# Sliding-window attention into a cosine-gated MLP on one core: register loads, the fifth half batch's key and query loads, w_out and three sets of casts placed elsewhere in the order

## The chip, the core and the metric

The kernel runs on one core of a Trainium2 chip. The metric is the device time of one execution in microseconds (us); the time of a kernel is the median of its runs. A profile is one execution more, recorded by the hardware profiler. Engines: PE (TensorE, matmuls; PEld is its weight load), DVE (VectorE), ACT (ScalarE), POOL (GpSimd, which also issues the DMAs that change the type) and SP (SyncE, which here issues DMAs only). Each engine works through its own instructions in the order in which they were written down.

## What is computed

Attention over 8 batches, 8 heads, 576 tokens and a head dimension of 64. A token sees its neighbours within 32 positions, and 8 global tokens see all and are seen by all. The result goes through an MLP whose hidden layer is multiplied by its own cosine.

```python
scores = scale * q @ k^T                       # where |i - j| <= 32, or i or j is global; else -1e9
attn   = exp(scores - max) / sum               # softmax
x      = (attn @ v), heads joined              # 4608 x 512
h      = x @ w_in                              # 512 -> 2048
out    = (h * cos(h)) @ w_out                  # 2048 -> 512, float32, 4608 x 512
```

## The kernel before

Work is cut into pairs of heads: 4 pairs make a batch, 2 a half batch, so there are 32 pairs and 16 half batches (s = 0 to 15; pair pr belongs to half batch pr // 2). The first five half batches (pairs 0 to 9) are loaded as they are and turned on PE; from half batch 5 on, keys, queries and values are first cast to fp16 in DRAM and then read with transposing DMAs. The MLP runs over 9 tiles of 512 tokens, each in 16 steps of the first product (four matmuls 128x512 into `ph`, L771, a cosine on ACT, L777, and a product on DVE that makes `g`, L778) and 16 steps of the second (four matmuls into `po`, L809).

**Who sets the order.** Nothing is scheduled by a tool: the order of every engine's instructions is written out by hand as strings of steps. FRONT holds the first five half batches; the loop then runs one round for each s from 4 on: MID for s = 4, FIFTH for s = 5, SIXTH for s = 6, ORDER for the others. A step calls one function, which appends its instructions to each engine that it uses. Steps that matter here, with what they issue:

- `sN`, `pN`, `xN`: scores of pair N (PE `st` L640, ACT `e` L643 and L647, DVE `pm` L644 and L648); values (PE `pv` L655, DVE `dg`, `r_all` and `xn`, L669 to L675); transposes of xn (PE `tx` L687, DVE `xT` and `xg`, L688 to L693), and after the fourth pair of a batch eight POOL copies of the global columns into xT (L696; L761 from pair 10 on), each at a column that a register holds. From pair 10 on the same steps are L708 to L717, L728 to L739 and L753 to L756. In the round strings, `sa`, `sz`, `pa`, `pz`, `xa`, `xz` are the two pairs of the round's half batch, and `kc qc`, `kd qd` bring the next half batch's keys and queries into `kw` and `qb` (L616, L628 on DVE).
- `kN qN` in FRONT: keys and queries of pair N turned on PE (L604) and copied by ACT (L613 to L625).
- `L4`: POOL issues the loads of half batch 4's keys and queries (L282, `kn` and `qn`). `M4`: SP issues its value rows (`vn`, L376, five loads, and two small ones, L381). `C2`, `C3`, `C4`: POOL casts the value rows of half batch 2, 3 or 4 into `vw` (L411, `cast_vn`). For s = 2 and 3 a one-element copy into `gate` comes first (L409): it reads the newest mask product `pm`. There are two buffers of `pm`, so the DVE product of the pair after the next has to wait for that copy.
- `I`: two iotas (L954, L955) and the reading of the eight global positions into POOL's registers (L956).
- `W0` to `W3`: POOL issues the four quarters of w_in (L902). `O`: w_out (L906), 2 MB in fp16, into a tile whose first part held keys and queries of half batch 2 until then. `H2`: a cast of the global values.
- `K5`, `K6`, `K7`: POOL issues the fp16 casts of half batch 5, 6 or 7 in DRAM (k and q at L273, v at L269). `V10`, `V12`: a one-element POOL copy (L398) that waits for `qb` of that pair and so holds back the casts behind it. From round 6 on, `G` does the same for later half batches (a copy that waits for xn, L988, then the casts).
- `B5`, and `bring(s + 2)` at the end of a round: SP issues the transposing loads of keys and queries (L287, L288), which wait for the casts, and the value loads into `vw` (L353 to L360, L423).
- `Z0` to `Z4`: DVE builds the mask of the later half batches in five parts; `Z5` clears the edges of `kT` and `qT`. `A0` to `A2`: gathers of the global rows on POOL (L338). `1` and `2`: one step of the MLP's first or second product; `m` and `t` are the two halves of a `1`. `f4`: four filling matmuls. `n`: a sum of squares on ACT (L827).

SP also stores each output block (L818), in the order in which the blocks and the `bring` steps were written. Three buffers hold blocks that wait for their store.

Of the kernel before, what the change touches and what calls it, by code (L numbers as in the profile page):

```python
# [20 lines left out]
NP = H // 2  # L21
# [25 lines left out]

ORDER = "2 kz qz sa 2 2 2 sz pa 1 2 1 2 xa n pz 1 1 G 2 xz 1 1 2 kc qc 1 1"

MID = ("+ 1 1 1 1 Z0 1 1 1 Z1 1 1 Z2 1 1 A0 1 Z3 1 1 1 n1 Z4 1 1 A1 1 1 1 Z5 A2 1 1 1 B5 1 2 2 g10 g11 kc qc V10 K6 n2 2 2 1 1 2 2 n3 kd qd - 2 2")  # L50

FIFTH = "sa G 2 2 2 2 sz pa 1 1 2 xa pz 2 2 2 kc qc V12 K7 xz n kd qd"

SIXTH = "sa 2 2 2 2 sz pa 1 1 2 xa 1 1 pz G 2 xz n 1 1 D0 2 kc qc D1 1 D2 2 1"

FRONT = ("M1 s0 E0 C0 E1 L2 w6 k1 q1 w4 s1 y0.0 f8 k2 q2 C1 H0 p0 M2 L3 y0.1 s2 k3 q3 f4 x0 p1 M3 s3 H1 g4 g5 g6 C2 g7 L4 I k4 q4 f4 x1 p2 M4 s4 "
         "C3 W0 k5 q5 f4 x2 p3 s5 g8 g9 W1 W2 W3 k6 q6 f4 x3 p4 s6 C4 k7 q7 f4 x4 p5 n0 s7 k8 q8 f4 x5 p6 s8 H2 k9 q9 f4 x6 p7 s9 "
         "x7 p8 O m m x8 K5 p9 t t + m m t t x9 -")
WARM = 13
KQ = 80  # L60
OK_ALL = float(P * (B * NP * 2 * BP + B))
# [144 lines left out]
def kernel(  # L206
# [189 lines left out]
    def hold(pr):  # L396

        nc.gpsimd.tensor_copy(gate, qb[pr % NK][0:1, 0, G : G + 1])  # L398

    def hold_x(pr):  # L400

        nc.gpsimd.tensor_copy(gate, xn_of[pr // 2][0:1, pr % 2, 0, 0:1])
# [2 lines left out]
        return view(vw[s % NV], (4 * (D + 1), NK5), (D + 1, 4), (1, D + 1))  # L405

    def cast_vn(s):
        if 1 < s < 4:
            nc.gpsimd.tensor_copy(gate, pm_of[max(pm_of)][0:1, 2 * CN - 1 : 2 * CN])  # L409
        old, new = vn_of(s).rearrange("p t (h d) -> p t h d", h=4), vn16(s)  # L410
        nc.gpsimd.tensor_copy(new[:, :, :, 0:D], old)  # L411
# [497 lines left out]
    with tc.manual_schedule():  # L909
# [85 lines left out]
        def bring(s):  # L995
# [4 lines left out]

        LOCAL = {"k": local_k, "q": local_q}
        OTHER = LOCAL | {"g": globals_kq, "L": load_qk, "W": load_w_in, "v": load_values, "n": x_squares,
                 "C": cast_vn, "I": row_numbers, "E": early_rows, "w": lambda n: warm(n, "h" if n == 6 else "s"), "y": value_rows, "M": next_values, "S": spread_vg, "V": hold, "U": hold_x, "H": early_globals, "Z": steady_buffers, "f": fill, "r": load_vn, "A": later_rows, "D": later_globals, "O": load_w_out, "K": lambda s: cast_half(s, "kqv"), "B": bring, "m": lambda _: one(False), "t": lambda _: mlp_act()}
        ready[0] = 1
        for step in FRONT.split():
            if step in "+-":
# [5 lines left out]
        for s in range(4, B * NP // 2):  # L1012
# [25 lines left out]
                        f(pr, *[int(x) for x in step[2:]])  # L1038
            if s % 2 == 1:
                ready[0] = s // 2 + 1 + (s // 2 == B - 1)  # L1040
            if 3 < s < B * NP // 2 - 2:
                bring(s + 2)
        x_squares(B * NP // 2 - 1)
        make_identity(nc, ident)
# [48 lines left out]
```

## Time and profile before

| | us |
|---|---|
| median of 3 runs (348.47 to 351.66) | 350.42 |
| the profiled execution | 351.74 |
| its span, first to last instruction | 349.9 |
| PE busy in the span | 328.1 |
| DVE busy | 249.7 |
| ACT busy | 238.3 |
| POOL busy | 106.1 |

The profile gives busy times of each engine, the waits with what ended them, a timeline, and the clock that PE was granted. The profiled execution took 351.74 us, of which 349.9 us are the span; 1.8 us lie around it. A row of a timeline reads: start in us, duration, engine, line, operation, out<-in, count, and in brackets how long the engine had been idle before it and what ended that.

### The profile page before, as it was taken

What the parts mean: (1) busy time and instruction counts of PE and PEld (TensorE: products, weight loads), DVE (VectorE), ACT (ScalarE), POOL (GpSimd) and SP (SyncE); (2) the same over time, 40 slices, a digit from 0 to 9 for tenths busy, and PEclk for the clock granted to TensorE, in tenths of its full rate; (3) what the DMA queues carried; (4) which work ended last, traced back from release to release, by engine and by line L of the source; (5) the groups of instructions that cost most, each with busy time, mean ns of one, the idle gap of its engine ahead of it and who ended that gap; (6) DMA issues with size and microseconds to landing.
All of it is one profiled execution on the core that took longest, in us unless ns stands there. A gap on an engine that the chain in (4) does not pass through costs nothing.

```text
span 349.9 us, 8348 instructions
## 1 busy us (share of the span) xinstructions
PE 328.1 (94%) x3153; PEld 170.9 (49%) x3153; DVE 249.7 (71%) x610; ACT 238.3 (68%) x411; POOL 106.1 (30%) x217
## 2 busy tenths in 40 slices
PE   6988589999998899999999999999999999999993
PEld 2567475444453345545454545454545444444452
DVE  6579768996575778888887978787888566556310
ACT  4887766885765686969687877778787866644300
POOL 7844737435043505250705071415001000000000
PEclk9999969999998999999999999999999999999997
DMA  5999995999999999999999999999990001100112
GB/s 86 195 151 166 176 204 71 197 179 94 209 98 181 156 175 130 186 131 164 165 199 147 184 135 182 139 182 142 178 130 7 30 32 51 39 33 30 60 62 68
DMA packets 165763, 45.00 MB, mean 129 GB/s; under 512 B 153060, under 2 KB 160868, under 8 KB 165540
## 3 DMA queue, kind: packets, MB, share of 16 engines
q1 hardware_dynamic: 106244, 26.86, 55.3%
q0 software_dynamic: 59472, 17.54, 49.3%
q8 instruction: 27, 0.44, 0.5%
q14 instruction: 20, 0.16, 0.2%
HBM read 44.93 MB, written 19.17 MB: 183 GB/s over the span
## 4 chain that ended last, share of the span: by engine, by line
PE 84%; DMA 4%; DVE 3%; ACT 3%; POOL 2%; issue 2%; SPq 1%; POOLq 0%; ACTq 0%
PE ph L771 36%; PE po L809 32%; PE pv L728 3%; PE st L708 2%; DMA qn<-in_q_dram 2%; PE tx L753 2%; PE pv L655 2%; DMA kn<-in_k_dram 2%; PE bank L604 1%; PE po L791 1%; PE pv L502 1%; PE tx L687 1%; PE st L640 1%; DVE g L778 1%; PE t L322 1%
## 5 line engine op out<-in xcount | busy, mean ns | idle before, releaser
L771 PE MATMUL ph<-xT,w_in 128*128 128x512 f16 x576 | 140.6, 383 | 2.5 <-POOL xT L761 1.7
L777 ACT ACTIVATE cos<-ph,pio 128x512 f16<-128x512 f32 x144 | 97.6, 687 | 61.2 <-PE ph L771 58.9
L809 PE MATMUL po<-w_out,g 128*128 128x512 f16 x560 | 136.9, 379 | 0.0
L778 DVE TENSOR_TENSOR g<-cos,ph 128x512 f16<-128x512 f16 x144 | 96.7, 686 | 47.5 <-ACT cos L777 44.9
L771 PEld LDWEIGHTS <-w_in 128*128 128x128 f16 x576 | 54.3, 98 | 64.5 <-issue 3.7
L809 PEld LDWEIGHTS <-g 128*128 128x128 f16 x560 | 53.7, 98 | 63.8 <-issue 0.6
L711 ACT ACTIVATE e<-st 128x512 f16<-128x512 f32 x44 | 23.9, 594 | 9.2 <-PE st L708 9.0
L712 DVE TENSOR_TENSOR pm<-e,mask 128x512 f16<-128x512 f16 x44 | 18.8, 429 | 13.5 <-ACT e L711 12.0
L988 POOL COPY gate<-xn 1x1 f16<-1x1 f16 x8 | 1.5, 182 | 82.3 <-DVE xn L739 82.3
L761 POOL COPY xT<-xg 128x4 f16 x48 | 17.2, 358 | 30.2 <-DVE xT L756 27.6
L273 POOL DMA_DIRECT2D q<-in_q_dram x11 | 24.3, 2212 | 0.0
L827 ACT ACTIVATE xn<-xn 128x1536 f16<-128x1536 f16 (+1 forms) x16 | 22.7, 1417 | 0.0
L739 DVE TENSOR_TENSOR xn<-pv,r_all 128x768 f16<-128x768 f32 x22 | 21.1, 958 | 1.0
L814 ACT COPY o<-po 128x512 f32<-128x512 f32 x17 | 10.0, 586 | 13.4 <-PE po L809 13.4
L816 DVE COPY o<-po 128x512 f32<-128x512 f32 x18 | 12.4, 690 | 9.2 <-PE po L809 8.7
L273 POOL DMA_DIRECT2D k<-in_k_dram x11 | 18.1, 1644 | 1.4 <-issue 1.4
L777 ACT ACT_TABLE_LOAD x12 | 15.4, 1283 | 0.2
L643 ACT ACTIVATE e<-st 128x488 f16<-128x488 f32 x20 | 10.6, 575 | 7.2 <-PE st L640 6.5
L711 ACT ACT_TABLE_LOAD x11 | 14.1, 1283 | 0.2
L644 DVE TENSOR_TENSOR pm<-e,qT 128x488 f16<-128x488 f16 x20 | 10.5, 551 | 4.8 <-issue 2.4
L708 PEld LDWEIGHTS <-kw 64*128 64x128 f16 x484 | 8.4, 95 | 9.9 <-issue 7.7
L588 POOL COPY kw<-kgT 128x88 f16<-128x88 f16 x22 | 12.7, 757 | 0.0
(182 smaller groups left out, 380.1 us busy)
## 6 DMA issues: line engine op xcount, KB each, us to landing
out_dram<-o SPq DMA_DIRECT2D x35, 256.0 KB
vw<-v SPq DMA_DIRECT2D x32, 165.0 KB
k<-in_k_dram POOLq DMA_DIRECT2D x11, 288.0 KB, 8.4
q<-in_q_dram POOLq DMA_DIRECT2D x11, 288.0 KB, 10.8
v<-in_v_dram POOLq DMA_DIRECT2D x11, 288.0 KB, 5.0
vn<-in_v_dram SPq DMA_DIRECT2D x20, 120.0 KB
w_in<-in_moe_w_in_dram POOLq DMA_DIRECT2D x4, 512.0 KB
w_out<-in_moe_w_out_dram POOLq DMA_DIRECT2D x1, 2048.0 KB, 15.5
```

Source lines behind the costliest of these rows:

```text
L273: nc.gpsimd.dma_start(dst[s].rearrange("t (h d) -> t h d", h=4), dview(src, base, (D, S), (S * D, 4), (1, D)))
L588: nc.gpsimd.tensor_copy(kw[pr % NK][:, :, 0:G], view(kgT[:, pr], (0, NB), (1, G)))
L708: nc.tensor.matmul(st[j // 8 * 2 + h][:, j % 8 * C : j % 8 * C + C], kp[hp, j], qp[hp, j], start=True, stop=True)
L711: nc.scalar.activation(e[:, 0:512], st[h], AF.Exp, scale=scale)
L712: nc.vector.tensor_tensor(view(pm[:, h], (1, 512)), e[:, 0:512], view(mask, (1, 512)), ALU.mult)
L739: nc.vector.tensor_tensor(view(xn, (384, 2), (D, 6), (1, D)), view(pv, (512, 2), (65, 6), (1, D)), view(rp, (6, 2), (1, 6), (0, D)), ALU.mult)
L761: nc.gpsimd.tensor_copy(xT[:, :, bass.ds(pool_idx[g] + b * S, 1)], xg[:, :, g : g + 1])
L771: nc.tensor.matmul(ph, w_in16[:, j, f * P : (f + 1) * P], xT[:, j, t * TT : (t + 1) * TT], start=(j == 0), stop=(j == NC - 1))
L777: nc.scalar.activation(cos, ph, AF.Sin, bias=pio2)
L778: nc.vector.tensor_tensor(g, cos, ph, ALU.mult)
L809: nc.tensor.matmul(po, g16[:, f, s * P : (s + 1) * P], w_out16[:, f], start=(f == 0), stop=(f == NF - 1))
L827: nc.scalar.activation(view(xn, (BP * P, 2), (1, n)), view(xn, (BP * P, 2), (1, n)), AF.Square, accum_out=x_sq[:, s : s + 1])
```

## The change

Only the order of steps changes, with one gate dropped and two swapped for gates on other tiles. No arithmetic is added.

- In FRONT, `I` and `L4` come ahead of `C2` (they stood behind it), and `C3` has no gate any more. `O` comes right behind `C4` and `H2`, ahead of the copies of batch 1's global columns; it stood behind them. `p7` comes ahead of `x6`.
- In MID, `Z5` and `B5` come 8 steps into the round instead of near its end; `Z4`, a new gate `N` that waits for the finished mask, and `K6` come ahead of the last seven first-product steps, where `V10 K6` stood behind `qc`. `B6` is written into MID, ahead of its last two pairs of `2`; it was issued at the end of the round.
- In FIFTH, `U10 K7` stands right behind `pa`: it waits for xn of pair 10. `V12 K7` stood behind `qc`, ahead of `xz`.
- In SIXTH, six steps trade places: a `2` comes ahead of the two `1` behind `pa`, one `1` moves from ahead of `pz` to behind it, and one to between `G 2` and `xz`.

```diff
-FIFTH = "sa G 2 2 2 2 sz pa 1 1 2 xa pz 2 2 2 kc qc V12 K7 xz n kd qd"
+FIFTH = "sa G 2 2 2 2 sz pa U10 K7 1 1 2 xa pz 2 2 2 kc qc xz n kd qd"
-SIXTH = "sa 2 2 2 2 sz pa 1 1 2 xa 1 1 pz G 2 xz n 1 1 D0 2 kc qc D1 1 D2 2 1"
+SIXTH = "sa 2 2 2 2 sz pa 2 1 1 xa 1 pz 1 G 2 1 xz n 1 D0 2 kc qc D1 1 D2 2 1"
...
+    def hold_mask(_):
+
+        nc.gpsimd.tensor_copy(gate, mask[0:1, 0, 0:1])
+
...
     def cast_vn(s):
-        if 1 < s < 4:
+        if s == 2:
             nc.gpsimd.tensor_copy(gate, pm_of[max(pm_of)][0:1, 2 * CN - 1 : 2 * CN])
...
-            if 3 < s < B * NP // 2 - 2:
+            if 4 < s < B * NP // 2 - 2:
                 bring(s + 2)
```

The first place is POOL in the front part, around the casts of the value rows of half batches 2 (`vw_94`) and 3 (`vw_95`). Before:

```order
L409 COPY gate<-pm 1x1
L411 CAST vw_94<-vn_118 128x20x64
L586 COPY kw_99<-kgT 128x5x8
L593 COPY qb_103<-qgT 128x4x8
L282 DMA kn_88<-in_k_dram 80x4x512
L282 DMA qn_90<-in_q_dram 80x4x512
L954 IOTA kid_i 128x11
L955 IOTA d_i 128x64
L956 TENSOR_LOAD gidx_row
L956 ISA x16
L409 COPY gate<-pm 1x1
L411 CAST vw_95<-vn_118 128x20x64
```

And in the changed kernel, from the same place (behind the copies for pair 6's globals):

```order
L958 IOTA kid_i 128x11
L959 IOTA d_i 128x64
L960 TENSOR_LOAD gidx_row
L960 ISA x16
L282 DMA kn_88<-in_k_dram 80x4x512
L282 DMA qn_90<-in_q_dram 80x4x512
L413 COPY gate<-pm 1x1
L415 CAST vw_94<-vn_118 128x20x64
L590 COPY kw_99<-kgT 128x5x8
L597 COPY qb_103<-qgT 128x4x8
L415 CAST vw_95<-vn_118 128x20x64
```

The iotas, the register load with its sixteen register instructions and the two loads of half batch 4 now stand between the copies and the first of the two casts; the second gate is gone, and the second cast follows the pair's copies directly.

The second place is POOL in round 5, around the casts of half batch 7 and the first of the eight copies of batch 2's global columns (each of them an ISA instruction for the address and a copy). Before:

```order
L398 COPY gate<-qb_100 1x1
L273 DMA k_80<-in_k_dram 2304x1x64
L273 DMA q_79<-in_q_dram 2304x1x64
L269 DMA v_81<-in_v_dram 16x9216
L761 ISA
L761 COPY xT<-xg 128x4
```

In the changed kernel:

```order
L406 COPY gate<-xn 1x1
L273 DMA k_80<-in_k_dram 2304x1x64
L273 DMA q_79<-in_q_dram 2304x1x64
L269 DMA v_81<-in_v_dram 16x9216
L765 ISA
L765 COPY xT<-xg 128x4
```

POOL's own order is the same here, but the gate in front now waits for xn of pair 10 instead of qb of pair 12, which DVE makes further on in the round.

The third place is DVE in round 6, from the values of pair 12 to the transposes of pair 13 (`g` is an MLP step, `xn` the end of a pair's values, `xg` and `xT` what follows its transposes). Before:

```order
L778 TENSOR_TENSOR g<-cos,ph 128x512 x2
L755 TENSOR_REDUCE xg<-tx 128x8
L756 COPY xT<-tx 128x616
L778 TENSOR_TENSOR g<-cos,ph 128x512 x2
L733 TENSOR_REDUCE dg<-pv 8x2
L734 RECIPROCAL r_all<-pv 128x12
L735 RECIPROCAL r_all<-dg 8x12
L739 TENSOR_TENSOR xn<-pv,r_all 128x768
L755 TENSOR_REDUCE xg<-tx 128x8
L756 COPY xT<-tx 128x616
L778 TENSOR_TENSOR g<-cos,ph 128x512 x2
```

In the changed kernel:

```order
L782 TENSOR_TENSOR g<-cos,ph 128x512 x2
L759 TENSOR_REDUCE xg<-tx 128x8
L760 COPY xT<-tx 128x616
L782 TENSOR_TENSOR g<-cos,ph 128x512
L737 TENSOR_REDUCE dg<-pv 8x2
L738 RECIPROCAL r_all<-pv 128x12
L739 RECIPROCAL r_all<-dg 8x12
L743 TENSOR_TENSOR xn<-pv,r_all 128x768
L782 TENSOR_TENSOR g<-cos,ph 128x512 x2
L759 TENSOR_REDUCE xg<-tx 128x8
L760 COPY xT<-tx 128x616
```

One `g` fewer stands ahead of pair 13's xn, and two `g` now stand between that xn and what the pair's transposes feed.

More of the change, by code (lines that the diff above doesn't have):

```diff
@@ L48 @@
 ORDER = "2 kz qz sa 2 2 2 sz pa 1 2 1 2 xa n pz 1 1 G 2 xz 1 1 2 kc qc 1 1"
[L50 to L58 removed]
+MID = ("+ 1 1 1 1 Z0 1 1 1 Z5 B5 1 Z1 1 1 Z2 1 1 A0 1 Z3 1 1 A1 1 n1 A2 g10 g11 1 Z4 N K6 1 1 1 1 1 1 1 2 2 kc qc n2 2 2 1 1 B6 2 2 n3 kd qd - 2 2")
+FIFTH = "sa G 2 2 2 2 sz pa U10 K7 1 1 2 xa pz 2 2 2 kc qc xz n kd qd"
+SIXTH = "sa 2 2 2 2 sz pa 2 1 1 xa 1 pz 1 G 2 1 xz n 1 D0 2 kc qc D1 1 D2 2 1"
+FRONT = ("M1 s0 E0 C0 E1 L2 w6 k1 q1 w4 s1 y0.0 f8 k2 q2 C1 H0 p0 M2 L3 y0.1 s2 k3 q3 f4 x0 p1 M3 s3 H1 g4 g5 g6 I L4 C2 g7 k4 q4 f4 x1 p2 M4 s4 "
+         "C3 W0 k5 q5 f4 x2 p3 s5 g8 g9 W1 W2 W3 k6 q6 f4 x3 p4 s6 C4 k7 q7 f4 x4 p5 n0 s7 k8 q8 f4 x5 p6 s8 H2 O k9 q9 f4 p7 x6 s9 "
+         "x7 p8 m m x8 K5 p9 t t + m m t t x9 -")
 WARM = 13
@@ L1002 @@
         OTHER = LOCAL | {"g": globals_kq, "L": load_qk, "W": load_w_in, "v": load_values, "n": x_squares,
-                 "C": cast_vn, "I": row_numbers, "E": early_rows, "w": lambda n: warm(n, "h" if n == 6 else "s"), "y": value_rows, "M": next_values, "S": spread_vg, "V": hold, "U": hold_x, "H": early_globals, "Z": steady_buffers, "f": fill, "r": load_vn, "A": later_rows, "D": later_globals, "O": load_w_out, "K": lambda s: cast_half(s, "kqv"), "B": bring, "m": lambda _: one(False), "t": lambda _: mlp_act()}
+                 "C": cast_vn, "I": row_numbers, "E": early_rows, "w": lambda n: warm(n, "h" if n == 6 else "s"), "y": value_rows, "M": next_values, "S": spread_vg, "V": hold, "N": hold_mask, "U": hold_x, "H": early_globals, "Z": steady_buffers, "f": fill, "r": load_vn, "A": later_rows, "D": later_globals, "O": load_w_out, "K": lambda s: cast_half(s, "kqv"), "B": bring, "m": lambda _: one(False), "t": lambda _: mlp_act()}
         ready[0] = 1
```

## The prediction

> **What bounds the kernel now.** I read the page first: who is busy, on which engine the chain that ended last lies, and PE's busy tenths in 40 slices of 8.75 us.
>
> ```profile
> PE 328.1 (94%) x3153; PEld 170.9 (49%) x3153; DVE 249.7 (71%) x610; ACT 238.3 (68%) x411; POOL 106.1 (30%) x217
> PE   6988589999998899999999999999999999999993
> PE 84%; DMA 4%; DVE 3%; ACT 3%; POOL 2%; issue 2%; SPq 1%; POOLq 0%; ACTq 0%
> ```
>
> PE bounds the whole, so an edit is worth what it takes out of PE's idle time and out of the time in which PE's clock is low. The slices under 9 are the front part, up to about 52 us, and two slices from 105 to 122; behind them nothing is to be won. Busy times by stretch (start:end, length, then busy time and count of PE, PEld, DVE, ACT, POOL, the granted clock, the DMA engines' share, GB/s) show a full stretch and the poor one.
>
> ```profile
> 58.00:79.00 21.00, 21.00 (x102) 9.71 (x101) 19.70 (x51) 17.24 (x27) 9.52 (x13) 1.00 1.40 180
> 105.00:120.00 15.00, 11.72 (x104) 5.36 (x96) 9.26 (x22) 8.58 (x15) 5.79 (x16) 0.89 1.57 180
> ```
>
> Of 105 to 120 PE is idle 3.3 us, and its clock is low besides. PE's own waits (who, for what: us, times, longest) name the places.
>
> ```profile
> PE st L640 <- DVE xg L693: 2.5, 1, 2.5
> PE ph L771 <- POOL xT L761: 1.7, 1, 1.7
> PE tx L753 <- DVE xn L739: 1.5, 1, 1.5
> ```
>
> The first is followed back in the timeline, POOL and DVE from 34 to 39 us.
>
> ```profile
> 34.56 0.65 POOL L282 DMA_DIRECT2D kn<-in_k_dram  x1
> 35.20 0.64 POOL L282 DMA_DIRECT2D qn<-in_q_dram  x1
> ...
> 38.12 0.18 POOL L409 COPY gate<-pm 1x1 f16<-1x1 f16 x1 [1.97 <-issue]
> 38.33 1.79 DVE L644 TENSOR_TENSOR pm<-e,qT 128x488 f16<-128x488 f16 x2 [1.96 <-POOL gate L409]
> 38.42 1.44 POOL L411 CAST vw<-vn 128x1280 f16<-128x1280 f32 x1
> ```
>
> DVE stands 1.96 us for `C3`'s gate, because POOL reads registers ahead of it, and PE then stands 2.5 us behind DVE. The change takes the register load and `L4` away from there and drops the gate.
>
> **Front part, the sum.** The register load now stands ahead of `C2`'s gate. Its pieces, then POOL's room there:
>
> ```profile
> L956 POOLq FUSED_REGOPS  x8: 147/147/191, 36.1 to 37.8; - x8
> L956 POOLq TENSOR_LOAD <-gidx_row x1: 2037/2037/2037, 34.0 to 34.0; - x1
> ```
>
> ```profile
> 27.78 0.18 POOL L409 COPY gate<-pm 1x1 f16<-1x1 f16 x1
> 32.51 1.28 POOL L411 CAST vw<-vn 128x1280 f16<-128x1280 f32 x1 [4.54 <-DMA vn<-in_v_dram]
> ```
>
> POOL idles 4.54 us between that gate and its cast. The load takes 2.04 us, its register operations run from 36.1 to 37.9, 1.8, and `L4`'s issues take 0.65 + 0.64: 5.1 us. From 27.8 this ends at 32.9; the load ran in the sequencer, from 34.0, ahead of issues that stand before it, so it may be half a microsecond earlier. The cast then starts at some 33.0 and not 32.51; pair 5's `pm`, which the gate holds, is about as late. I charge 0.5 once, between 0 and 0.7.
>
> What the stretch takes undisturbed comes from the ends of the pairs' values on DVE (`xn`); with them the first `pm` of pair 5, pair 4's values on PE, and a sum of squares on ACT.
>
> ```profile
> 28.32 0.82 DVE L675 TENSOR_TENSOR xn<-pv,r_all 128x640 f16<-128x640 f32 x1
> 31.49 0.82 DVE L675 TENSOR_TENSOR xn<-pv,r_all 128x640 f16<-128x640 f32 x1
> 32.27 1.79 DVE L644 TENSOR_TENSOR pm<-e,qT 128x488 f16<-128x488 f16 x2
> 33.84 1.03 PE L655 MATMUL pv<-vw,pm 128*128 128x65 f16 x20 [0.72 <-POOL vw L411]
> 35.55 0.82 DVE L675 TENSOR_TENSOR xn<-pv,r_all 128x640 f16<-128x640 f32 x1
> 38.05 1.33 ACT L827 ACTIVATE xn<-xn 128x1280 f16<-128x1280 f16 x1
> 56.90 0.82 DVE L675 TENSOR_TENSOR xn<-pv,r_all 128x640 f16<-128x640 f32 x1
> ```
>
> One undisturbed pair takes 31.49 - 28.32 = 3.17 us. Pairs 3 and 9 end at 31.49 and 56.90: six pairs in 25.41, where 6 x 3.17 = 19.0 would do, 6.4 less (the half clock behind PE's stall included). Of that the new order does not win the 0.9 by which pair 4 is long already (35.55 - 31.49 = 4.06, PE waiting for `C2`'s cast), nor the 0.5 above, nor what the squares cost, which the gate's wait hides now: between 0 and 1.33, and as ACT's exponentials feed the next `pm`, I take 0.8. Remainder 6.4 - 0.9 - 0.5 - 0.8 = **4.2**; 5.5 if neither costs anything.
>
> The low end is set by `L4`'s transfers, which now run while half batch 3's value rows arrive. Loads of that kind from POOL's queue (q0) against SP's (q1), in the 3 us from 25 to 28, where `L3` ran and two of SP's value loads were issued:
>
> ```profile
> q0 software_dynamic: 565, 0.56, 115.5%
> q1 hardware_dynamic: 24, 0.01, 1.3%
> ```
>
> SP's rows stand meanwhile. `L4` is 2 x 320 KB, 3.4 us at 0.56 MB in 3 us, so `C3`, which ends at 39.86 now, could end 3.4 later, at 43.3. Pair 6's values are due at 35.55 + 0.5 + 2 x 3.17 + 0.8 - 1.7 = 41.5 (pair 4's began 1.7 ahead of its xn): 1.8 late, 2.4 left. I keep 4.2, as most of those rows are under way before `L4`'s first bytes, some 2 us behind its issue.
>
> **105 to 120, the sum.** DVE and POOL around 100 us:
>
> ```profile
> 100.39 0.47 DVE L756 COPY xT<-tx 128x616 f16<-128x616 f16 x1
> 100.49 0.18 POOL L398 COPY gate<-qb 1x1 f16<-1x1 f16 x1 [13.06 <-DVE qb L628]
> 103.63 3.74 POOL L761 COPY xT<-xg 128x4 f16 x8
> ```
>
> POOL sat idle 13.06 us, then issued `K7` at the moment when DVE had the columns ready (100.86), and copied them only at 103.63 to 107.37. With `K7` behind `pa` the copies can start at 100.9 and end at 104.6; PE waits for them for 1.7 us, so from 105.7, and that goes. With it goes a stretch at half clock:
>
> ```profile
> 39.17:42.58 3.41, 0.74 (x20) 0.46 (x20) 3.34 (x10) 2.33 (x7) 3.41 (x8) 1.00 1.23 208
> 42.58:45.99 3.41, 3.14 (x45) 2.89 (x45) 1.60 (x6) 1.16 (x3) 2.46 (x10) 0.50 1.32 195
> 104.02:107.43 3.41, 1.66 (x49) 1.05 (x48) 3.06 (x10) 2.89 (x8) 2.98 (x11) 1.00 2.07 146
> 107.43:110.85 3.42, 3.42 (x9) 1.19 (x9) 1.71 (x3) 1.20 (x2) 0.71 (x4) 0.50 1.70 249
> 114.26:117.67 3.41, 1.92 (x21) 0.92 (x15) 2.57 (x8) 1.83 (x3) 0.76 (x3) 1.00 1.38 187
> ```
>
> In steps of 3.41 us, PE was busy 0.74 and 1.66 us in the two that a low one follows, and 1.92 in one that the low clock does not follow: under about half busy, and the next step runs at 0.50. Without its wait PE is busy all through 104.02:107.43, so 3.41 x 0.5 = 1.7 us come back. The third wait, 1.5 ahead of pair 13's `tx`, is covered by the sixth round's new order: a `1`, a `2` and a `1` stand between its values and its transposes, 2.5 us at 0.82 each (21.00 / 102 x 4), where now a `2` and the wait make 2.3. Sum 1.7 + 1.7 + 1.5 = 4.9. Against it I set 0.7: behind `pa` two `1` now follow each other while ACT loads its cosine table, and PE has two `ph` buffers for them; less than the 1.5 that such a wait on DVE costs now. **4.2**; ends 2.5 (the low clock stays and the new waits cost as much as I charge) and 4.9.
>
> The Trainium skill, "TensorE: Matmul & The Clock Gate", Part 1, has the clock fall after an idle window of about 3.4 us. The step agrees with this trace, the condition does not: 104.02:107.43 was half busy. By the page a wait of 1.7 us would not be the cause of the low clock, and the second sum would be 2.5.
>
> **Edits at nothing.** `O`, and `K5` behind it, come sooner by as much as the front or more; their users `po`, `kT` and `qT` come sooner by the front's 4.2, so their cover stays. `Z5` is DVE work that is only moved, and `B5` waits on SP for `K5` as before. `p7` and `x6` wait for the same xn. If SP loses its place over `B6` or `K6`, that is the second rival.
>
> **Sum.** 4.2 + 4.2 = 8.4. The profiled execution took 351.74 (span 349.9), so one like it would take 343.3. The median of the runs stands 1.3 lower, at 350.42: **342.0**. A measurement of this kernel tells about 1% (3.5 us) from no change.
>
> **Rivals.**
>
> Half of it (0.18): one stretch does not give. The nearest way is that the wait moves from `C3`'s gate to `C2`'s, or half batch 3's rows come late, and the front gives nothing: 350.42 - 4.2 = 346.2. For it: POOL's room of 4.54 us is less than the 5.1 us of work put there. Against it: DVE needs the gate only at 32.27.
>
> Stores behind transposes (0.10). `B6` now stands behind the first output block instead of the second.
>
> ```profile
> 90.43 2.33 SPq L287 DMA_TRANSPOSE kT<-k  x1
> 104.78 0.92 SPq L818 DMA_DIRECT2D out_dram<-o  x2
> 104.92 0.68 DVE L816 COPY o<-po 128x512 f32<-128x512 f32 x1
> ```
>
> `B6` holds SP from 90.43 to 104.78. Three buffers hold blocks, and the fifth block's copy (104.92) needs the second's store, which goes out at once now. With `B6` some 6 us sooner (its casts no longer wait for `qc`) that store is out at 98.8 and the copy, at 100.7, has its buffer. If `K6` collides with `B5`'s loads and `B6` stays at its place, DVE and PE stand 104.8 + 2 - 100.7 = 6 us and pay 1.7 of low clock: 342.0 + 7.7 = 349.7.
>
> Slower (0.10): half batch 4's value rows starve under w_in. By the queue rows above, loads of SP that are not yet under way stand while POOL's run. They wait for half batch 3's, which `L4` now delays to about 39; w_in is issued when `C3` is through.
>
> ```profile
> w_in<-in_moe_w_in_dram POOLq DMA_DIRECT2D x4, 512.0 KB
> 52.12 1.03 PE L655 MATMUL pv<-vw,pm 128*128 128x65 f16 x20
> ```
>
> If w_in (issue 40.3, first bytes 2 us later) is first, it holds them for 2.0 MB at 0.56 MB in 3 us, 11 us, to 53. `C4` then ends at 54.7 and pair 8's values, at 52.12 now, follow 2.6 later; PE, idle since pair 7, runs two steps at half clock, 3.4 more. The front loses 6.0, the second stretch still gives 4.2: 352.2, and over 354 if `K5`, late as well, makes pair 10 wait. It decides by a microsecond: whether the last rows are asked for before about 41.
>
> The Trainium skill, "DMA: Bandwidth & Descriptors", "Queues, rings and completion order", has each DMA engine go round between the queues that have work. By that the rows would only be slowed and this rival would have no chance; the 1.3% speaks against it for loads not yet begun.
>
> That the change does nothing (0.04), neither gate having held PE: 350.4.
>
> **Chances.** Forecast 0.58, half 0.18, stores 0.10, slower 0.10, nothing 0.04. The forecast's own range is 350.4 - 5.5 - 4.9 = 340.0 to 350.4 - 2.4 - 2.5 = 345.5. To hold 8 in 10, and with a microsecond for the runs' scatter (348.47 to 351.66 before), it takes in the half case: 339.0 to 347.5. Faster by over 1% (below 346.9): the forecast and nearly all of the half case, 0.75; within 1%: the rest of it, the stores, nothing, and half of the slower rival, 0.20; slower by over 1%: 0.05.
>
> **What would show it.** Right: no DVE wait for a gate at 38 us, and at most 0.7 us at pair 5's `pm`; pair 9's xn at 52 to 53 us; a granted clock of 1.00 from 38 to 50 and from 104 to 111; PE's waits for POOL `xT` and DVE `xn` gone. Wrong: `C4`'s cast waiting for `vn` past 47 us; PE behind a DVE `o`; a low step of the clock behind a step more than half busy; a wait on `kT` or `vw` behind 79 us that is not there now.

## The result, and the profile after

| | before | changed |
|---|---|---|
| median of 20 runs each, us | 350.46 | 348.92 |
| ratio, 95% interval | | 0.9948 (0.9926 to 0.9970) |
| the profiled execution, us | 351.74 | 347.20 |
| its span, us | 349.9 | 345.5 |

In 15 of its 20 runs the changed kernel is 0.5% faster, 1.8 us (1.0 to 2.6), where 8.4 were forecast; the other five took 355 to 360 us and are not in the ratio, and with them its mean is 350.1 against 350.5 before, so that nothing is left of the gain. A second comparison gave 0.9926 (0.9900 to 0.9952) without four of 12 runs, which took 351.6 to 357.5.

The page of the changed kernel, busy time of PE and its tenths in 40 slices:

```profile
PE 326.8 (95%) x3153; PEld 170.3 (49%) x3153; DVE 249.5 (72%) x610; ACT 237.9 (69%) x411; POOL 107.0 (31%) x216
PE   6977979999999999999999999999999999999993
```

The two poor slices behind 105 us are gone; the front part still has a six and sevens. Stretches of the changed kernel (columns as in the prediction): the one from 105 on, and three steps of the clock in the front:

```profile
105.00:120.00 15.00, 13.67 (x111) 6.33 (x109) 10.97 (x25) 10.88 (x21) 4.97 (x8) 1.00 1.65 123
31.91:35.32 3.41, 1.62 (x49) 1.42 (x43) 2.02 (x3) 2.68 (x7) 3.08 (x6) 1.00 1.25 175
35.32:38.74 3.42, 3.42 (x61) 2.63 (x58) 3.17 (x12) 1.98 (x5) 0.22 (x1) 0.50 1.24 208
38.74:42.15 3.41, 3.41 (x55) 2.82 (x54) 2.24 (x8) 3.00 (x7) 1.12 (x1) 0.50 1.05 159
```

From 105 to 120 PE idles 1.3 us where it idled 3.3, at full clock. The front again has a step in which PE works half the time and two at half clock behind it, 7 us earlier than before. PE's waits in the changed kernel name the new place:

```profile
PE pv L659 <- POOL vw L415: 1.8, 1, 1.8
PE t L568 <- ACT g L557: 0.8, 1, 0.8
...
PE st L712 <- DVE qb L632: 0.6, 1, 0.6
```

The waits for `xg` (2.5), `xT` (1.7) and `xn` (1.5) are gone or down to 0.2; pair 4's values now wait 1.8 for the third cast. POOL's timeline of the changed kernel shows why, and DVE's `pm` of pair 5 what else hangs there:

```profile
27.90 0.17 POOL L959 IOTA d_i<- 128x64 int32 x1
32.24 0.64 POOL L282 DMA_DIRECT2D kn<-in_k_dram  x1 [4.17 <-PE bank L608]
32.87 0.64 POOL L282 DMA_DIRECT2D qn<-in_q_dram  x1
33.62 1.25 POOL L415 CAST vw<-vn 128x1280 f16<-128x1280 f32 x1
33.71 1.76 DVE L648 TENSOR_TENSOR pm<-e,qT 128x488 f16<-128x488 f16 x2 [1.39 <-POOL gate L413]
41.03 1.26 POOL L415 CAST vw<-vn 128x1280 f16<-128x1280 f32 x1 [5.49 <-DMA vn<-in_v_dram]
42.23 0.76 POOL L906 DMA_DIRECT2D w_in<-in_moe_w_in_dram  x1
48.77 1.25 POOL L415 CAST vw<-vn 128x1280 f16<-128x1280 f32 x1
```

The three casts read in order: `C2` at 33.62 (32.51 before), `C3` at 41.03 (38.42), `C4` at 48.77 (46.47). Between the iotas and `L4`'s first issue lie 4.17 us. The bracket names PE, but the gap is the register load: it is 4.17 or 4.18 in all six traces of this order, one of which names another PE instruction. Its pieces in the changed kernel:

```profile
L960 POOLq FUSED_REGOPS  x8: 147/147/195, 29.4 to 31.5; - x8
L960 POOLq SEQ_ASSERT  x8: 18/18/32, 29.7 to 31.7; - x8
L960 POOLq TENSOR_LOAD <-gidx_row x1: 2032/2032/2032, 27.3 to 27.3; - x1
```

The load starts half a microsecond ahead of the iotas and ends at 29.3; the register operations take until 31.7, and `L4`'s first issue comes 0.5 later. `C3`'s rows are late because `L4`'s 640 KB run in the middle of them: from 34 to 38 us POOL's queue moved 0.62 MB and SP's 0.16.

### The profile page after: what moved, and what is told of

It is laid out like the page before. It is cut to its first block, busy times and chain, and to the rows that moved or that the text cites. A ratio compares the mean times of both kernels' runs of the same rounds, so it can differ in the third digit from the quotient of the medians.

```text
span 345.5 us, 8346 instructions
## 1 busy us (share of the span) xinstructions
PE 326.8 (95%) x3153; PEld 170.3 (49%) x3153; DVE 249.5 (72%) x610; ACT 237.9 (69%) x411; POOL 107.0 (31%) x216
## 3 DMA queue, kind: packets, MB, share of 16 engines
q0 software_dynamic: 59472, 17.54, 51.8%
## 4 chain that ended last, share of the span: by engine, by line
PE 81%; DVE 5%; ACT 5%; DMA 3%; issue 2%; SPq 1%; POOL 1%; ACTq 0%; POOLq 0%; DVEq 0%
PE po L813 33%; PE ph L775 32%; PE pv L732 3%; PE st L712 2%; PE pv L659 2%; DVE g L782 2%; PE tx L757 2%; DMA kn<-in_k_dram 2%; DMA vw<-vg 2%; PE bank L608 2%; PE st L644 1%; ACT cos L781 1%; PE po L795 1%; PE pv L506 1%; SPq L427 1%
## 5 line engine op out<-in xcount | busy, mean ns | idle before, releaser
L781 ACT ACTIVATE cos<-ph,pio 128x512 f16<-128x512 f32 x144 | 97.5, 686 | 59.3 <-PE ph L775 56.8
L765 POOL COPY xT<-xg 128x4 f16 x48 | 15.3, 319 | 31.0 <-DVE xT L760 28.4
L592 POOL COPY kw<-kgT 128x88 f16<-128x88 f16 x22 | 13.4, 788 | 0.0
```

Source lines behind the costliest of these rows:

```text
L592: nc.gpsimd.tensor_copy(kw[pr % NK][:, :, 0:G], view(kgT[:, pr], (0, NB), (1, G)))
L765: nc.gpsimd.tensor_copy(xT[:, :, bass.ds(pool_idx[g] + b * S, 1)], xg[:, :, g : g + 1])
L781: nc.scalar.activation(cos, ph, AF.Sin, bias=pio2)
```

## Experiments: where the front's gain went

Two theories at the start: the stall was moved (M), or the front gave its 4.2 us and something behind took them back (P). One measure serves all: the end of pair 9's xn, the last pair of the front.

### Each half of the change alone

```diff
# the kernel before, front edit alone
-... g4 g5 g6 C2 g7 L4 I k4 ...        if 1 < s < 4:
+... g4 g5 g6 I L4 C2 g7 k4 ...        if s == 2:
# the changed kernel, that edit undone: the same lines the other way round
```

> The kernel before with the front edit alone: register load and half batch 4's loads ahead of the third value cast, no gate at the fourth. Theory M (the stall is moved, not removed): pair 4's values wait 1.5 to 2 us for that cast, two steps at half clock follow from about 35 us, and pair 9's xn ends 1 to 2 us sooner than 56.9; time 349 to 350.5, ratio 0.996 to 1.000. Theory P (the front gives its 4.2 us and something later in the changed kernel takes it back): no such wait here, pair 9's xn at 52 to 53; ratio 0.988. Theory S (the new front brings a slower clock to some executions and nothing else): ratio 1.000 or above.

> The changed kernel with the front edit undone (the load, half batch 4's loads and both gates as before), so the other edits alone. Theory M: the front as before (2.5 us of PE wait, half clock from 42.6), the stretch from 105 to 120 full and at a clock of 1.00; 3 to 3.5 us below the kernel before in the trace from po on, time 347 to 348, ratio 0.990 to 0.993. Theory P: the same 4.2 us that the front gives are lost here, so no gain: ratio 1.000. Theory H (the half clock step at 107 us that the change removes is not in every execution of the kernel before, so the median holds less than the trace shows): ratio 0.994 to 0.998.

The front edit alone: 0.9977 (0.9942 to 1.0012), the 1.8 us wait for the cast there, half clock from 34.9 to 41.8 and once more from 52.0 to 55.4, pair 9 at 58.1; two of its 12 runs took 353.9 and 355.7. Everything but the front edit: 0.998 (0.9947 to 1.0012) by the ratio, 348.42 against 349.93 in the medians, pair 9 at 55.9, with the old front, whose wait for `xg` was 1.1 us here and not 2.5. So the new front gave nothing in that execution, and the old one reached, by itself, what the changed kernel had shown (55.8). P falls; M holds for its mechanism, though not for its number (pair 9 was to come 1 to 2 us sooner). The intervals are too wide to rank the halves; from here on the traces' stretches do that.

### Which of the moves makes the cast late

```diff
-... g4 g5 g6 I L4 C2 g7 k4 ...
+... g4 g5 g6 I C2 g7 L4 k4 ...     # loads back behind the cast
+... g4 g5 g6 L4 C2 g7 I k4 ...     # register load back behind it
```

> The changed kernel with half batch 4's two loads back behind the third value cast; the register load stays ahead of it and the fourth cast has no gate. Theory M1 (the two loads delay the cast: they wait for their buffer until 32.2 and take 1.3 us): the cast begins at 31.8 to 32.4, pair 4's values wait under 0.5 us, no step at half clock before 50 us, pair 9's xn at 51 to 53; 2.5 to 4 us below the changed kernel, 345 to 346.5. Theory M2 (the register load is enough to make the cast late): the cast still begins past 33, wait and half clock as in the changed kernel; within 0.5 us of it. Theory M3 (the value rows are late whatever stands there, behind half batch 4's loads): pair 6's or 7's values wait for the fourth cast and the half clock comes some us later; within 1.5 us of it.

> The changed kernel with the register load back behind the third cast; half batch 4's loads stay ahead of it, the fourth cast has no gate. Theory L (the loads alone delay the third cast, as they wait for their buffer until 32.2): cast at 33.4 to 33.8, PE's wait of 1.5 to 2 us for it and the half clock behind it as in the changed kernel, fourth cast at 41 to 42, time within 1 us of the changed kernel's. Theory I (the register load does): cast at 32.3 to 32.8, PE's wait under 1 us, no half clock step right behind it; the fourth cast still at 40 or later because of the rows.

> The changed kernel with the register load behind the third cast, once more and with more rounds. Theory F: pair 9's xn at 55 to 56 and ratio 0.991 to 0.994, better than the changed kernel on the same chip. Theory Z: pair 9's xn anywhere from 55 to 58, ratio 0.994 to 0.998.

Loads back: 0.9968 (0.9936 to 0.9999), 5 of 12 runs over 353, and the profile has the fifth cast at 50.24, pair 9 at 59.7. POOL's timeline of that run:

```profile
28.95 0.17 POOL L959 IOTA d_i<- 128x64 int32 x1
32.83 0.44 POOL L413 COPY gate<-pm 1x1 f16<-1x1 f16 x1 [3.71 <-issue]
33.22 1.25 POOL L415 CAST vw<-vn 128x1280 f16<-128x1280 f32 x1
37.02 1.26 POOL L415 CAST vw<-vn 128x1280 f16<-128x1280 f32 x1 [1.02 <-DMA vn<-in_v_dram]
38.21 0.76 POOL L906 DMA_DIRECT2D w_in<-in_moe_w_in_dram  x1
50.24 1.27 POOL L415 CAST vw<-vn 128x1280 f16<-128x1280 f32 x1 [5.60 <-issue]
```

The register load alone still holds POOL for 3.7 us and the cast starts past 33, as M2 had it, with M3's late values on top. But PE's wait for that cast is 1.1 us, no half clock follows it before 51, and M1 does not fall: from the second iota to the cast it is 4.3 us here and 5.7 in the changed kernel, so the two loads add 1.4, and this execution reached the iota 1 us later, behind half clock from 23.7 to 30.5. From 27.9 the same 4.3 us would end at 32.2, inside M1's range. With the register load behind the cast, in the second of the two such runs:

```profile
28.30 0.64 POOL L282 DMA_DIRECT2D kn<-in_k_dram  x1
...
29.56 0.18 POOL L413 COPY gate<-pm 1x1 f16<-1x1 f16 x1
32.72 1.25 POOL L415 CAST vw<-vn 128x1280 f16<-128x1280 f32 x1 [2.98 <-DMA vn<-vg]
34.61 0.13 POOL L958 IOTA kid_i<- 128x11 int32 x1
38.68 1.25 POOL L415 CAST vw<-vn 128x1280 f16<-128x1280 f32 x1 [3.81 <-DMA vn<-vg]
39.88 0.76 POOL L906 DMA_DIRECT2D w_in<-in_moe_w_in_dram  x1
46.52 1.25 POOL L415 CAST vw<-vn 128x1280 f16<-128x1280 f32 x1
```

`L4` goes out at 28.3 and not at 32.2, so its buffers were free all the time, the cast waits for its rows and for nothing else, and the register load costs nothing where it stands, in POOL's wait for the next rows. PE's wait for the cast: 1.2 and 0.4 us in the two runs; pair 9 at 55.6 and 55.0. Ratios 0.9959 (0.9916 to 1.0001) and 0.9930 (0.9896 to 0.9963). Theory I, for the wait, though 1.2 is over the 1 us that it allowed and the fourth cast came at 39.7 and 38.7, not at 40 or later; of theory L stays that the rows can be up to 0.7 us later (cast at 33.2 in the first of the two). Neither trace has half clock between 20 and 48 us. The second meets theory F's numbers (55.0, 0.9930).

### The gate alone

```diff
# the changed kernel with the old front order; gate at s == 2 only
+... g4 g5 g6 C2 g7 L4 I k4 ...
# and, in the second run, all of w_in together and later
-... C3 W0 k5 q5 f4 x2 p3 s5 g8 g9 W1 W2 W3 ...
+... C3 k5 q5 f4 x2 p3 s5 g8 g9 W0 W1 W2 W3 ...
```

> The changed kernel with the front's old order (third cast, then half batch 4's loads, then the register load), only the fourth cast's gate left out. Theory G (in the front the gate was the whole cost; the two moves are what spoils it): DVE does not stand at 38 us, PE's wait of 1 to 2.5 us for xg is gone, no cast is later than in the kernel before (32.5, 38.4, 46.5, each within 0.7), pair 9's xn ends at 54 to 55.5; time 346 to 347.5, ratio 0.989 to 0.993. Theory N (behind the gate another wait of the same length comes up: the value rows, or ACT): pair 9's xn at 55.8 to 57.5 as with the gate; 348 to 349. Theory R (the fourth cast, no longer held, sends w_in off ahead of half batch 4's value rows): fifth cast past 49, pair 8 or 9 late by 3 us or more, 350 or above.

> The kernel without the gate and with the old front order, and the first quarter of w_in behind the copies for pairs 8 and 9, so all four quarters go out together some 1 to 1.5 us later. Theory R (value rows of half batch 4 starve when w_in is asked for first): fifth cast at 45 to 47 in every execution, few executions over 350, time at or below that of the kernel with w_in in its old place. If w_in is not in the way there: the same time within 0.5 us. If w_in is itself late then: PE waits for w_in at the first ph, 1 us more.

Ratios 0.9950 (0.9923 to 0.9977) and 0.9951 (0.9916 to 0.9986), fifth cast at 45.1 in both, pair 9 at 58.1 and 55.9. PE's longest wait behind the casts, in the first (2.2 in the second):

```profile
PE bank L608 <- DMA qn<-in_q_dram: 1.8, 1, 1.8
```

The stall on DVE is gone, and 2 us of waiting for half batch 4's queries stand in its place: theory N. That is the load which the change brings forward. So there were two waits one behind the other, and a third, for the cast, that appears when the loads come first with the register load ahead of them. R did not occur; w_in's place made no difference here.

### The order that takes out all three

```diff
-... g4 g5 g6 I L4 C2 g7 k4 ... C3 W0 k5 q5 f4 x2 p3 s5 g8 g9 W1 W2 W3
+... g4 g5 g6 L4 C2 g7 I k4 ... C3 k5 q5 f4 x2 p3 s5 g8 g9 W0 W1 W2 W3
# and, in a further run, the copies of pairs 8 and 9 right behind g7:
+... g4 g5 g6 L4 C2 g7 g8 g9 I k4 ...
```

> The changed kernel with the register load behind the third cast (half batch 4's loads stay ahead of it) and the first quarter of w_in behind the copies for pairs 8 and 9. Without that last edit PE waited 1.1 us for those copies, which stood behind w_in's issue. Theory F (each wait taken out of the front is time won): pair 9's xn at 53.5 to 55, time 345 to 347, 1 us or more below both the kernel before and the changed kernel. Theory Z (the front's end is set by the waits that come up behind and by the clock of the execution): pair 9's xn between 55 and 59, time 347 to 349, level with the changed kernel.

> The run with half batch 4's loads first, the register load behind the third cast and w_in later, once more with more rounds. Theory F: ratio 0.988 to 0.991, pair 9's xn at 55 to 56. Theory Z: ratio 0.993 or above.

> As in the run with the loads first and w_in later, and the copies for pairs 8 and 9 moved from behind the fourth cast to where POOL idles for that cast's rows (35 to 39.6). Theory F: PE's wait of 1.1 to 1.2 us ahead of pair 8's scores at 42 goes, pair 9's xn at 54 to 55, a further 0.5 to 1 us. Theory Z: pair 8 then waits for its values or the xT copies instead, pair 9's xn at 55 to 56, the same time.

0.9894 (0.9843 to 0.9945; 5 of 6 runs, without one of 350.8) and 0.9915 (0.9878 to 0.9952; 7 runs), pair 9 at 55.8 and 57.2. It is faster than the kernel before; against the changed kernel, whose better runs gave 0.9926 beside the first of these, the intervals overlap. The two theories are not told apart: the first run has F's time and Z's pair 9 (F had 53.5 to 55, and the wait of 1.1 to 1.2 before pair 8's scores stayed), and the second has a ratio between theirs and pair 9 behind F's 55 to 56. But none of its 13 runs, nor of the 22 with only the register load moved, took more than 350.8 us. The early copies were a miss: 1.0110 (1.0072 to 1.0147). PE stood 4.9 us for `qb` from 29.5:

```profile
PE st L644 <- POOL qb L597: 4.9, 1, 4.9
```

There are four buffers of `kw` and `qb`, so pair 8's copies go into the buffer from which pair 4's scores read. Written ahead of these scores and behind the third cast, they hold them back, and they put pair 8's global columns in the place of pair 4's. So this run is no test of F.

### The same kernels once more

> The changed kernel once more, for another execution of the same instructions. Theory Z: the steps at half clock lie elsewhere (the grid of 3.41 us starts elsewhere), pair 9's xn anywhere from 55.5 to 59; from the 25th to the 41st product g 50.3 again and from the 49th on 202.2 to 202.4 again, so all that scatters lies in the front. Theory Q (the front is 1.9 us shorter for good): pair 9's xn at 55.5 to 56.2.

> The kernel before once more, for another execution. Theory Z: pair 9's xn between 55.5 and 59; from the 25th to the 41st product g 51.4 if no step at half clock follows PE's wait of 1.75 us at 105, 53.1 if one does; the two waits there as before. Theory Q: pair 9's xn at 57 to 58.

The changed kernel: wait 1.8 for the cast and half clock from 34.8 to 41.6 again, pair 9 at 55.9. The kernel before: pair 9 at 56.8, not 57.7, and no step at half clock behind the wait at 105. The theories meet here: the order of waits repeats, where pair 9 ends does not quite. All ends, with the rows in time:

| front | pair 9's xn ends, us |
|---|---|
| old order, both gates (5 traces) | 57.7, 55.9, 57.2, 57.7, 56.8 |
| the change (3) | 55.8, 58.1, 55.9 |
| old order, gate left out (2) | 58.1, 55.9 |
| loads ahead, register load behind (4) | 55.6, 55.0, 55.8, 57.2 |

Means 57.1, 56.6, 57.0, 55.9: the change gained some 0.5 us, less than the traces of one order differ among themselves. In three of these traces (55.9 and 57.2 of the old order, the last 57.2) pair 3 was already 1.7 to 4.6 us later than in the kernel before; without them the means are 57.4, 56.6, 57.0 and 55.5. The order with the register load behind is then the only one of which every trace lies below every trace of the old order; for the change as it stands no gain of the front is shown.

## Experiments: the runs at 355 us

Filling matmuls in PE's wait were to tell the wait from the clock behind it:

```diff
-... k6 q6 f4 x3 p4 ...
+... k6 q6 f4 x3 f18 p4 ...
```

> The changed kernel with 18 filling matmuls (0.08 us each, 1.45 us) ahead of pair 4's values, where PE idles 1.8 us for the third cast; the wait itself stays. Theory C (what the late cast costs is the clock behind it): no two steps at half clock from 35 us, pairs 5 to 8 1 to 3 us sooner than in the changed kernel (42.3 to 42.8, 45.6, 48.6, 53.0), pair 9's xn at 53 to 54.8, time 1 to 2.5 us below the changed kernel's. Theory D (in that stretch the pairs wait for other work anyway, the value rows of the fourth cast first, so the clock costs little): no half clock there either, but pair 9's xn at 55.3 to 56.5 and the time within 0.7 us of the changed kernel's.

0.9919 (0.9887 to 0.9950). Seven runs under 350 had a mean clock of 0.987 to 0.996 and a median of 347.22; eight of the changed kernel (second comparison) 0.982 to 0.994 and 346.98. The two sets are from different chips; the ratios to the kernel before are 0.9919 and 0.9926. The mean clock came up a little, the time did not go down: theory D, on times alone, as the profiled execution was the one at 355.57, and it has a step at half clock from 40.4 to 43.8. Kept traces give D's price. Pairs 4 to 7 (ends of xn) took 10.8, 11.5 and 11.5 us in the three traces of the change, with two steps at half clock there, and 10.3, 10.0 and 10.3 in three with the register load behind and no such step: about 1 us, where two steps at the 1.70 of the MLP rounds (below) would make 3.4. The profile at 355.57 shows what such a run is. POOL:

```profile
29.88 0.17 POOL L959 IOTA d_i<- 128x64 int32 x1
34.22 0.64 POOL L282 DMA_DIRECT2D kn<-in_k_dram  x1 [4.17 <-PE bank L608]
35.61 1.25 POOL L415 CAST vw<-vn 128x1280 f16<-128x1280 f32 x1
...
37.12 1.25 POOL L415 CAST vw<-vn 128x1280 f16<-128x1280 f32 x1
38.32 0.76 POOL L906 DMA_DIRECT2D w_in<-in_moe_w_in_dram  x1
...
55.62 1.25 POOL L415 CAST vw<-vn 128x1280 f16<-128x1280 f32 x1 [11.35 <-issue]
```

and SP's loads of half batch 4's rows, with PE behind the fifth cast:

```profile
38.38 3.97 SPq L376 DMA_DIRECT2D vn<-in_v_dram  x5
56.93 1.54 PE L659 MATMUL pv<-vw,pm 128*128 128x65 f16 x20 [3.98 <-POOL vw L415]
```

Half batch 4's rows go into the buffer that the third cast empties. PE was 2 us late by half clock from 20.0 to 26.8, POOL's copies with it, and from there the register load and the loads follow in one row, so the third cast moved from 33.6 to 35.6. The fourth cast's rows had arrived by then; it came 1.5 us behind the third, and w_in went out at 38.32, just before the rows were asked for. The queues from 39 to 53 us in this run, and from 38 to 42 in the changed kernel's trace (packets, MB, share of 16 engines):

```profile
q0 software_dynamic: 2033, 2.02, 88.7%
q1 hardware_dynamic: 2445, 0.62, 27.3%
```

```profile
q1 hardware_dynamic: 2613, 0.66, 103.3%
q0 software_dynamic: 47, 0.04, 6.0%
```

The same rows take 14 us beside w_in and 4 alone. That is the prediction's slower rival. Two runs asked whether the dropped gate lets it in:

```diff
# gate back:                 # w_in later:
-        if s == 2:          -... C3 W0 k5 ... g8 g9 W1 W2 W3
+        if 1 < s < 4:       +... C3 k5 ... g8 g9 W0 W1 W2 W3
```

> The changed kernel with the gate in front of the fourth cast put back (it waits for the newest pm); all else as changed. Theory V (without that gate the fourth cast can follow the third at once, w_in then goes out at 38 while half batch 4's value rows are still being asked for, and these take 14 us instead of 4): no execution above 352, where the changed kernel had 5 of 20 and 4 of 12; the fourth cast not before 38, w_in not before 39; median within 0.7 us of the changed kernel's other executions. Theory K (those executions come from the clock, which falls to 0.96 to 0.97 in them, and not from an order of transfers): as many above 352 as in the changed kernel, a fifth to a third.

> The changed kernel with the first quarter of w_in behind the copies for pairs 8 and 9, the gate left out as in the change. Theory V: w_in goes out 1 to 1.5 us later, at 39.3 or later where the casts follow each other at 37; half batch 4's rows, asked for from 38.4 to 42.4, are then partly ahead: executions above 352 get fewer or shorter (349 to 353 in place of 355 to 360). Theory K: as many and as long.

Both profiles show it again. POOL in the run with the gate back:

```profile
33.87 0.64 POOL L282 DMA_DIRECT2D kn<-in_k_dram  x1 [4.17 <-PE tx L691]
35.26 1.25 POOL L415 CAST vw<-vn 128x1280 f16<-128x1280 f32 x1
37.58 1.25 POOL L415 CAST vw<-vn 128x1280 f16<-128x1280 f32 x1
38.78 0.76 POOL L906 DMA_DIRECT2D w_in<-in_moe_w_in_dram  x1
54.20 1.25 POOL L415 CAST vw<-vn 128x1280 f16<-128x1280 f32 x1 [8.87 <-issue]
```

4 of 12 runs over 352 with the gate, 3 of 10 with w_in later (354.0 to 356.1; w_in at 39.5 in its trace, still with the fifth cast at 54.2): theory V falls in its cause, and K in its own, since the transfers are what is late. Both these traces, and the one with the loads behind, again have half clock early in the front (24.9 to 31.7, 22.6 to 26.0, 23.7 to 30.5 us); the three of the change with the rows in time have none between 8 and 34. With the register load behind, half clock from 22.5 to 32.8 did no such harm: third cast at 32.7, fifth at 47.3. So in these traces it takes both, the early half clock and the register load ahead of the cast; that every run over 354 is of this kind is not shown, as the others were not profiled. What goes with it is the time from the third cast to w_in's issue:

| | third cast, w_in, fifth cast, us |
|---|---|
| before | 32.5, 39.8, 46.5 |
| changed | 33.6, 42.2, 48.8 |
| register load behind (second run) | 32.7, 39.9, 46.5 |
| loads behind | 33.2, 38.2, 50.2 |
| gate back | 35.3, 38.8, 54.2 |
| w_in later | 35.5, 39.5, 54.2 |
| filling matmuls | 35.6, 38.3, 55.6 |

With some 7 us between the first two, or more, the rows are in time, with 5 partly, with 4 or less not. Of the kernels with the register load ahead of the third cast 18 of 86 runs took over 354 us; with it behind, and the later edits made, none of 71 (the early copies apart).

## Experiments: the later rounds

```diff
# the kernel before with one of these alone
+FIFTH = "sa G 2 2 2 2 sz pa U10 K7 1 1 2 xa pz 2 2 2 kc qc xz n kd qd"
+SIXTH = "sa 2 2 2 2 sz pa 2 1 1 xa 1 pz 1 G 2 1 xz n 1 D0 2 kc qc D1 1 D2 2 1"
```

> The kernel before with round 5's edit alone: half batch 7's casts behind pair 10's values. If this edit is what takes away PE's wait for the eight copies of the columns (1.75 us) and the half clock step behind it (1.7): from the trace 3.4 us less, 347.1, ratio 0.990, and the wait of 1.5 for pair 13's xn still there. If the wait goes but the half clock step comes anyway (theory C: it hangs on the wait for xn behind it): 1.7 less, 348.8, ratio 0.995. If the wait only changes its place (theory W: the copies end sooner, PE is then held by g or by xT from DVE): ratio 0.998 to 1.002.

> The kernel before with the sixth round's new order alone. By the prediction's term the wait of 1.5 us ahead of pair 13's transposes goes and 0.7 or less comes in its place: from the 25th to the 49th product g 0.8 to 1.5 us less than in an execution of the kernel before with the same steps of the clock (68.0 without a half clock step there, 69.8 with one); the wait of 1.75 for the copies stays. If the new order only moves the wait (ACT's table loads, g): less than 0.4. Time 0.1 to 0.4% below before.

The times gave 0.998 (0.9948 to 1.0012) and 0.9967 (0.9929 to 1.0004). The traces are sharper. From the 25th to the 41st product `g`: 53.1 us before, 51.4 before once more and with the front edit alone, 50.8 with round 5's edit, 50.4 with round 6's, 50.3 in all fourteen traces with both; from the 49th to the end all take 202.0 to 202.4, but for two traces with a late value transfer (the second trace of the kernel before is one). The first and the last of these stretches, and between them the kernel before once more; ahead of that its step of the clock at 104 us:

```profile
77.90:131.00 53.10, 49.07 (x450) 23.42 (x448) 35.06 (x79) 35.48 (x63) 16.84 (x32) 0.97 1.57 153
```

```profile
104.15:107.56 3.41, 1.66 (x32) 1.05 (x29) 3.08 (x8) 2.86 (x6) 2.66 (x11) 1.00 1.76 241
77.00:128.40 51.40, 47.37 (x449) 23.08 (x448) 34.86 (x80) 35.46 (x63) 16.84 (x32) 1.00 1.47 156
```

```profile
76.10:126.40 50.30, 47.95 (x451) 23.21 (x450) 35.12 (x79) 35.54 (x63) 15.48 (x31) 1.00 1.62 148
```

The two of the kernel before differ by 1.70 us, all of it PE busy time (49.07 against 47.37, idle 4.03 in both): this is the half clock's price, as forecast, but one of three traces with that wait paid it. The changed kernel idles 2.35 instead of 4.03 there and gains 1.1 in length; PE's busy time is 0.6 longer, for which no run gives the reason. The stretch for which round 6's run was forecast ends at the 49th product: 68.05 before once more, 67.5 with round 5's edit, 67.6 with round 6's, 67.0 with both. So round 5's wins 0.6 and round 6's 0.5, not the 0.8 to 1.5 expected of it, and together they are 1.1; the 1.0 that round 6's seems to win up to the 41st is half given back by the 49th. Round 5's takes the wait for `xT` away, round 6's the wait for xn and, against what was expected, 1.0 of the 1.75 for `xT`. Each wins less than the waits that it removes, since others come up: for ACT's copy of the globals (0.8, above; its tile is named `g` too), for `qb` (0.6) and for the MLP's `g` (0.4). So it is neither W nor the full sum.

## Why the prediction was wrong

The two profiled executions differ by 4.4 us of span: 1.9 up to pair 9's xn, 2.75 from the 25th to the 41st `g`, and -0.2 elsewhere. Part of that is luck: the kernel before had drawn a late front and the half clock step at 107 in that execution, and against the other traces 0.5 and 1.1 are left.

**The front, forecast 4.2, came to about 0.5.** The step that failed is the charge "I charge 0.5 once, between 0 and 0.7" for the later `C2`. Its working gave a cast at 33.0; it came at 33.6, 1.1 later than before. The load did start half a microsecond ahead, as allowed for, but the register operations took 2.3 us and not 1.8, and 0.5 more passed before `L4`'s first issue, which the sum did not have. But the size is the smaller error. The charge took the delay as one that shifts a cast, not as the end of a chain: behind it stand PE's 1.8 us for pair 4 (0.7 before), pair 5's `pm` (1.39 for the gate, where 32.27 was due) and two steps at half clock. With the register load behind the cast this wait is 1.2 and 0.4 and that half clock is gone, which shows the cause. The wait moved, which the prediction had as its first rival ("the wait moves from `C3`'s gate to `C2`'s, or half batch 3's rows come late"); both happened.

That step is not all that is missing: without it, with the register load behind the cast, the front gains 1.9 in the mean (57.4 to 55.5), not 4.2. The 6.4 us were read off one execution at the late end (57.7 of 55.9 to 57.7), and the best trace (register load behind the cast) takes 22.1 us from pair 3's xn to pair 9's, where the sum had 25.4 - 4.2 = 21.2. What pairs 4 to 7 win, the last two pairs give back in part: pair 7's xn ends at 48.6 after against 51.8 before, pair 9's only 1.9 sooner; in that best trace at 46.9 and 55.0, 4.9 and 2.8 sooner. From pair 7's values to pair 8's it is 2.9 us before, 4.1 after and 3.8 there; PE idles 0.6 for POOL's copies into xT and 0.65 for ACT's `e` in both. Whether these are what holds pairs 8 and 9 was not tried.

**`L4` against half batch 3's rows.** Kept as a bound ("could end 3.4 later, at 43.3"), not charged; the fourth cast ended at 42.29, 2.4 later than before. That was right in kind. PE has no wait for this cast in the three traces of the change, where the half clock had made it late as well, so what the delay costs alone is not shown.

**105 to 120, forecast 4.2.** The two waits went, as said, and no step at half clock follows. Against the profiled execution 2.75 came, inside the term's own ends of 2.5 and 4.9. The term was mis-sized: the clock's 1.7 is its price only in the executions that pay it (one of three), and of the 3.25 us of waits removed 2.2 came back, 1.6 as new waits and 0.6 as longer work, where 0.7 was charged. Sure are 1.1.

**The slower rival** had 0.10, at 352.2; the runs over 354 are longer than that. Its mechanism is shown, with rows that share the engines with w_in and a fifth cast at 54 to 56, in three traces. It came true in some executions and not in others, which one forecast for all executions couldn't say; what lets it in is the register load in the third cast's chain, with an early half clock, not `C3` alone. The Trainium skill, "DMA: Bandwidth & Descriptors", "Queues, rings and completion order", has each DMA engine go round between queues at packet granularity. From 47 to 51 us of the run with filling matmuls this holds to a tenth (q0 first, then q1), and the inference drawn from it, that the rival then had no chance, was the mistake: with equal turns, 256 byte packets beside 1 KB ones get a fifth of the bytes.

```profile
q0 software_dynamic: 634, 0.63, 92.5%
q1 hardware_dynamic: 581, 0.14, 27.8%
```

**Stores behind transposes** did not happen: neither PE nor DVE waits for a DVE `o` or for a store in any trace. "Edits at nothing" held: from pair 9's xn to the 25th `g` 20.3 us after, 20.2 before.

**The clock.** "Under about half busy, and the next step runs at 0.50" does not hold: 1.66 us busy at 104 was followed by half clock in one trace of the kernel before and by full clock in the other. The steps stand on a grid that starts elsewhere in each execution; with the front edit alone the same wait lay across two steps, 2.85 and 2.24 us busy, and none fell. The Trainium skill, "TensorE: Matmul & The Clock Gate", Part 1, says that the window runs free of the kernel's start, and the traces agree; what decides between 1.66 and 1.66 stays open.

## What to carry to other kernels

An idle stretch ahead of an instruction is room only if what is put there starts on time: work moved in front of a cast joins everything behind it to everything ahead, so add up the whole chain from its last sure event, and again with that event 2 us later. Where a wait goes, name the next thing that is due (here half batch 4's queries, for which PE stood 1.8 to 2.2 us with the gate gone, then the cast) and price it from the same trace before counting the gap as won. A gap in one execution is one draw: read the same stretch in two or three traces before charging it, and look at single runs before believing a ratio.

## Unexpected about the hardware

- Reading eight registers left POOL without work for 4.17 to 4.18 us in six traces, of which the load itself, begun ahead of the iotas, takes only the first 1.3; where POOL had copies and two issues to do during the load, 1.97 were left.
- Two DMA queues with work got nearly equal numbers of packets (634 to 581 in 4 us), so the queue with 256 byte packets fell from 0.66 MB in 4 us to 0.62 in 14.
- Two steps at half clock in the front stand beside about 1 us lost there, and one in the MLP rounds cost 1.70 us.
- The name in a wait's bracket can be wrong: the 4.17 us of the register load are put down to two different PE instructions.
